# An mLSTM cell and a tanh-shrink MLP on one core: the filler matmuls before the first scores, and the densities in a list schedule

## The chip, the cores and the metric

The kernel runs on one core of a Trainium2 chip. The time is device microseconds of one execution, and the number compared is the median over several runs. A profiled execution has a span (first to last instruction) and a time of its own that is a little longer.

## The reference

First an mLSTM cell over 768 steps, for 4 sequences with 8 heads of 40 features; its output, 3072 tokens of 320 features, then goes through an MLP with 2048 hidden features whose activation is h - tanh(h).

```python
# q, k, v, o_gate: (4, 8, 768, 40); i_gate, f_gate: (4, 8, 768)
for t in range(S):
    m_new = maximum(f_gate[t] + m, i_gate[t])
    f_stab, i_stab = exp(f_gate[t] + m - m_new), exp(i_gate[t] - m_new)
    C = f_stab * C + i_stab * outer(v[t], k[t])        # (B, H, D, D)
    n = f_stab * n + i_stab * k[t]
    denom = maximum(abs(n . q[t]), 1.0)
    y[t] = sigmoid(o_gate[t]) * (C q[t]) / denom
x = y.transpose(0, 2, 1, 3).reshape(3072, 320)
h = x @ w_in                                            # (320, 2048)
out = (h - tanh(h)) @ w_out                             # (2048, 320)
```

## The kernel before

**The cell.** The 768 steps are cut into six chunks of 128, so with four sequences there are 24 units; unit n is chunk n // 4 of sequence n % 4. Each unit goes through the same operations. `scores` are 8 products of kz and qz into the PSUM banks `a0` and `a1`. VectorE masks them into P (two operations, tile `P`). `second` is 8 products of P with the scaled values vs (tile `ph`), and from the second chunk on also three products with the carried state. `gate` divides by the denominator and multiplies with the sigmoid of o (tiles `den`, `o`, `ys`). `turn` transposes the unit's y on TensorE (tile `px`), ScalarE copies it into xT, and `update` makes the new state from k and vs (tile `pc`). The gate sequences of the first two chunks are made ready first: a scan on VectorE, four transposes on TensorE and two products with triangles of ones (tile `gate`).

**The MLP.** Two units make a group of 256 tokens, and w_in and w_out are cut into eight pairs of blocks. They are stored in 64 bits and are converted on VectorE and ScalarE (tiles `w_e`, `w_m`, `w_r`). An item is one or two (group, pair) combinations: `ph_up` products with w_in, the activation on ScalarE and VectorE (tiles `z`, `q`, `gt`), and the way down (`po`, or `pS` in a form with seven products).

**The order.** Twelve units, the conversions and the MLP items of the first four groups are ordered by a list scheduler in the kernel's own text, the class `Plan`. Each `plan.add` gives an operation an engine, an assumed duration, what it comes after, a rank, tokens for buffers and banks, and a density `dense`. The order it finds is fixed on TensorE, VectorE and ScalarE: each instruction is chained behind the one before it on its engine. The DMA queue of SyncE (SP) isn't chained. There the framework places the transfers, and every transfer also waits for the one that used its completion semaphore eight before it, so that at most eight transfers of SP and ScalarE together are under way. From unit 12 on the order is a fixed pattern.

**Ones.** A matrix of ones (`diag`, bf16) is used for filler: `awake` and `stream` issue 128x512 matmuls whose result nobody reads. When `Plan.run` finds TensorE idle between two operations, `idle` fills the gap with as many as fit by the planner's clock. `share` adds up the densities of what TensorE did in the last `SPAN` us; when an operation of low density would bring this under `FEW`, denser work is taken first or ones are put in. `COLD` is the planner's assumption on how long TensorE runs slowly at the start.

**The loads.** For units 0 and 1 the loads stand ahead of everything else. The loads of later units are operations of engine "S" in the plan. The transfer of kz for unit 2 has one more wait: it goes behind the last TensorE instruction that had been recorded when the planner reached it.

```python
u[name] = plan.add("S", us, lambda: [load_unit(n, (name,), behind=[T.last] if n == 2 and name == "kz" else ()), arrive(n)], of(*after) + of(n - 1, name), rank + LATE.get(name, 0.0) + 2.0 * (n < 2), at=6.0 + 8.0 * (n < 2), kb=kb)
```

Of the kernel before, what the change touches and what calls it, by code (L numbers as in the profile page):

```python
# [79 lines left out]
def kernel(  # L80
# [77 lines left out]
    class Plan:  # L158
# [4 lines left out]
        LAG = {"T": 0.25, "V": 0.07, "A": 0.12, "S": 1.7, "G": 1.9, "N": 1.7}  # L163
        RATE, SHARED, COLD, TURN, WAIT = 0.3, 28.0, (12.0, 1.8), 0.12, 0.0364
        FEW, SPAN = 0.48, 2.6

# [176 lines left out]


    probe = const.tile([128, 1], FP, name="probe")
    V.memset(probe, 0.0)
# [5 lines left out]
    ones = const.tile([128, TOP], FP, name="ones")  # L352
    diag = const.tile([128, H, L], BF, name="diag")
# [10 lines left out]
    V.memset(ones, 1.0)  # L364
    V.memset(diag[:, HH:H], 1.0)

# [567 lines left out]
    PLANNED = 12  # L934
    SCALED, SHARED = (2, 4, 5, 6, 7, 11), (2, 4, 5, 6, 10, 11)
    RANKS = (-1.0, -1.0, -0.9464, 0.1262, 2.0044, 0.8216, 4.0244, 3.1226, 4.4155, 7.4293, 5.3654, 7.7018)
    WEIGHTS = (0.08, 0.0673, 1.9556, 3.3287, 6.8826, 8.3015, 4.4893, 6.619)
    START = item(FIRST * NP)
    HOLD = 32.6427
    plan = Plan(small=("b0", "b1"), a=1, up=1, po0=1, po1=1, gt=2, z=1, s4=1, P=4, vs=4, w64a=2, w64b=2, w=2, ob=2)  # L940

    def gates(c0, c1, rank, at, banks_of, after=()):
# [10 lines left out]
        def add(engine, us, name, after, take=None, give=None):  # L953
# [41 lines left out]
    units = {}  # L995
    LATE = {"o": -0.0338, "k": -2.3312}

    def plan_unit(n, rank):
# [26 lines left out]
        def first_part():  # L1025
# [9 lines left out]
        u["mask"] = [plan.add("V", 0.62, lambda i=i: ready[1][i](), [u["scores"]], rank - 0.621, give=[("a", held)] if i else ())  # L1035
                     for i in range(2)]
# [14 lines left out]
        for j, heads in enumerate(parts):  # L1051
            op = plan.add("T", 0.223 * len(heads) + (0.22 if c else 0.0), lambda j=j, heads=heads: second_part(j, heads),
                          ([op] if op else [u["prep"], u["column"], *before, *of(n, "q2") * (c > 0)]) + (u["mask"] if c else u["mask"][j:j + 1]), rank,
                          take=() if op else [("small", held)], give=[("P", held)] if j == len(parts) - 1 else (), dense=0.35)
        u["second"] = op
        if shared:
            steps = []
            over = plan.add("V", 0.6, lambda: [steps.extend(gate(n, in_parts=True)), steps[0]()], [op], rank - 1.4012)
            shares = plan.add("A", 1.9, lambda: steps[1](), [over, u["open"]], rank + 0.9389)
            u["gate"] = plan.add("V", 0.5, lambda: steps[2](), [shares, *of(n - 2, "turn")], rank - 3.6979, give=[("small", held)])  # L1060
        else:
# [15 lines left out]
        u["x"] = plan.add("A", 0.5, lambda: keep_x(n), [u["turn"]], rank - 3.4037, give=[("small", held_x)])  # L1077
        late = rank + (2.5552 if c else 1.5639)
# [6 lines left out]
    def plan_weights(p, rank, at):  # L1085
        for k, block in enumerate(blocks_of(p)):
            fetch, parts, low, power, one, sign, product = block
            held, r, buffer = {}, rank + 0.7421 * k, "w64" + "ab"[k]
            op = plan.add("G", 0.6 if k else 2.2, lambda fetch=fetch: fetch(begun[-1:]), begun_in_plan[:], r, [(buffer, held)], at=at, kb=655)
# [7 lines left out]

    plan.free["T"] = 1.6
    plan_gates(0, -2.0, 3.2, in_small)
# [4 lines left out]
    for n in range(2, PLANNED):  # L1104
        if n == 2 * B:
            plan_gates(1, 4.0679, 30.0, in_po)
        plan_unit(n, RANKS[n])
# [5 lines left out]
    for p in range(SPLIT, NP):  # L1113
        steps = []
        op = None
        for i in range(2):
            op = plan.add("V", 0.65, lambda p=p, i=i, steps=steps: [steps.extend([] if i else sums_of_weights(p)), *[step() for _, step in steps[2 * i:2 * i + 2]]],
                          [op] if op else [converted[p, 1], *([made[p - 1]] if p % 2 else [converted[n, k] for n in range(1, NP) for k in range(2)])], 0.2073 + 1.0 * p)
        made[p] = op

    def plan_item(x):

        run_of, some = items[x], tuple(run[:2] for run in items[x])
        n, rank = len(some), 2.2103 + 0.4005 * x
        held, got = {}, []
# [21 lines left out]

        op = plan.add("T", 0.43 * n, rest, [op], rank, tiles=2)

# [7 lines left out]
        for i in range(2):  # L1157
            z.append(plan.add("A", 0.3 + 0.25 * n, lambda i=i: square(i), [op, *z], -2.8126, () if i else [("z", held), ("gt", held)]))
        q = [plan.add("A", 0.2 + 0.25 * n, lambda i=i: got[2][1](i), [z[i]], -0.4608) for i in range(2)]
        cube = [plan.add("V", 0.15 + 0.27 * n, lambda i=i: got[2][2](i), [z[i]], -6.2574, give=[("up", held)] if i else ()) for i in range(2)]  # L1160
        g = [plan.add("V", 0.15 + 0.27 * n, lambda i=i: got[2][3](i), [q[i], cube[1]], -3.6973, give=[("z", held)] if i else ()) for i in range(2)]
        shrunk = g
        seven, (group, pair) = in_seven(*some[0]), some[0]
        if seven:
            g = [plan.add("V", 0.8 * n, lambda: sums_of_g(some), g[-1:], -3.0, [("w", held), ("s4", held)])]
        if x == START - 1:
            return
        if seven:
# [15 lines left out]
            for k, (cost, do, need) in enumerate(((0.82 * n, begin_run, [*shrunk, *sums_ready]),  # L1184
                                                  (0.54 * n, lambda: [step() for _, step in steps[3 * n + 1:5 * n + 1]], g),
                                                  (0.54 * n, lambda: [step() for _, step in steps[5 * n + 1:7 * n + 1]], []))):
                downs.append(plan.add("T", cost, do, need + downs[-1:] + [converted[p, 1] for _, p in some], rank + 0.4226,
                                      [("po0", mine), ("po1", mine), (name, mine)] if k == 0 and pair == SPLIT else (),
# [7 lines left out]
        for k, run in enumerate(run_of):  # L1196
            product, evict = down(k, some, *run, evict_at_once=False)
            first, last = run[1] == run[2], run[1] == run[3]
            for tt in range(GT):
                key = (run[0], run[2], tt)  # L1200
                po_held = runs.setdefault(key, {})
                done = plan.add("T", 1.08, lambda tt=tt, product=product: [product(i, tt) for i in range(2)],
                                g + downs[-1:] + [converted[run[1], 1]] + ([po_held["last"]] if "last" in po_held else []), rank + 0.4226,
                                [(f"po{tt}", po_held)] if first else (), [("gt", held)] if k == n - 1 and tt == GT - 1 else ())
# [275 lines left out]
```

## Time and profile before

| what | value |
|---|---|
| median of three runs | 544.16 us (542.82, 544.16, 552.6) |
| profiled execution, its own time | 542.34 us |
| its span | 540.1 us |
| mean granted TensorE clock | 0.982 |
| TensorE matmuls busy | 530.6 us, 98% |
| VectorE busy | 351.0 us, 65% |
| ScalarE busy | 200.7 us, 37% |
| matmuls of ones (`awake`) | 21, of which 18 before the first `ph_up` |
| first `ph_up` | at 27.22 us |

The table is read from the top down: TensorE is nearly always busy, so the span is the sum of what it does, of the few gaps in it and of the time in which its clock was lower. A matmul of float32 shows as two rows (two passes), so that 8 products are "x16".

### The profile page before, as it was taken

The page shows a single profiled execution, that of the slowest core. Times are in us where ns is not written, and L with a number is a line of the kernel's source. Part 1 is how long each engine was busy: PE and PEld are TensorE (multiplying, and loading weights), DVE is VectorE, ACT ScalarE, POOL GpSimd, SP SyncE. Part 2 cuts the span into 40 slices and gives each one's busy share as a digit, 9 for nine tenths or more (in the row PEclk, how much of TensorE's full clock was granted, in tenths as well). Part 3 has the DMA queues.
Part 4 walks back from the last instruction along what each step waited for, and adds up shares of the span by engine and source line. Part 5 has one row for each costly group of instructions (what it writes and reads, how often), then busy time and mean ns, then how long its engine had stood idle before and what let it go on. Part 6 is the DMA issues. An engine that isn't in the chain of part 4 may idle for free.

```text
span 540.1 us, 9214 instructions
## 1 busy us (share of the span) xinstructions
PE 530.6 (98%) x3475; PEld 461.9 (86%) x3475; DVE 351.0 (65%) x758; ACT 200.7 (37%) x534; POOL 26.9 (5%) x51
## 2 busy tenths in 40 slices
PE   7999999999999999999999999999999999999995
PEld 5788888888888989889999998998899899888873
DVE  5599999999764757855753854755655646553421
ACT  4458777454523423223213312322242242232321
POOL 4320212100000000000000000000000000000000
PEclk8599999999999999999999999999999999999999
DMA  7977653631001202021220310210200000000000
GB/s 226 278 236 224 208 169 103 184 100 53 13 1 37 62 26 76 27 64 32 81 53 24 92 58 26 74 50 26 72 16 12 1 25 0 2 25 0 26 0 30
DMA packets 28043, 37.98 MB, mean 70 GB/s; under 512 B 3736, under 2 KB 21720, under 8 KB 27992
## 3 DMA queue, kind: packets, MB, share of 16 engines
q1 hardware_dynamic: 21296, 22.24, 14.0%
q0 software_dynamic: 3040, 10.82, 6.5%
q10 hardware_dynamic: 3656, 4.26, 2.3%
q8 instruction: 29, 0.48, 0.4%
q14 instruction: 22, 0.18, 0.1%
HBM read 33.37 MB, written 3.93 MB: 69 GB/s over the span
## 4 chain that ended last, share of the span: by engine, by line
PE 98%; DMA 1%; SPq 0%; DVE 0%; issue 0%; ACT 0%; DVEq 0%
PE ph_up L130 41%; PE pS L130 26%; PE ph L130 10%; PE po L130 10%; PE ps L130 4%; PE pc L130 2%; PE px L134 2%; PE awake L130 1%; DMA kz<-in_kT 1%; PE gate L130 0%; SPq L303 0%; DVE P L107 0%; PE gate L134 0%; ACT ob L107 0%; SPq L322 0%
## 5 line engine op out<-in xcount | busy, mean ns | idle before, releaser
L130 PE MATMUL ph_up<-xT,w_in 128*128 128x256 f32 (+1 forms) x1152 | 245.0, 391 | 0.1
L130 PEld LDWEIGHTS ph_up<-xT,w_in 128*128 128x128 f32 (+1 forms) x1152 | 169.1, 189 | 29.2 <-issue 12.1
L107 ACT ACTIVATE z<-ph_up 128x512 f32<-128x512 f32 (+1 forms) x98 | 56.8, 584 | 261.8 <-issue 147.3
L107 DVE SCALAR_TENSOR_TENSOR gt<-ph_up,z 128x512 f32<-128x512 f32 (+1 forms) x98 | 62.6, 674 | 76.9 <-ACT z L107 76.9
L107 DVE TENSOR_TENSOR P<-ps,upto 128x512 f32<-128x512 f32 x48 | 31.6, 683 | 66.8 <-PE ps L130 66.7
L130 PE MATMUL pS<-wT,s 128*128 128x160 f32 x432 | 65.8, 300 | 0.0
L130 PEld LDWEIGHTS ph<-vs,P 128*128 128x128 f32 x384 | 60.6, 202 | 5.3 <-issue 0.9
L107 ACT ACTIVATE q<-z,tiny 128x512 f32<-128x512 f32 (+1 forms) x98 | 64.7, 709 | 0.0
L107 DVE SCALAR_TENSOR_TENSOR gt<-q,gt 128x512 f32<-128x512 f32 (+1 forms) x98 | 62.7, 672 | 0.2 <-ACT q L107 0.2
L130 PEld LDWEIGHTS pS<-wT,s 128*128 128x128 f32 x432 | 60.8, 190 | 0.0
L130 PE MATMUL ph<-vs,P 128*128 128x41 f32 x384 | 58.6, 272 | 0.0
L130 PE MATMUL po<-w_out,gt 128*128 128x320 f32 x192 | 56.4, 440 | 0.0
L130 PE MATMUL pS<-w_out,gt 128*128 128x160 f32 x288 | 51.1, 310 | 0.0
L130 PEld LDWEIGHTS po<-w_out,gt 128*128 128x128 f32 x192 | 35.0, 190 | 14.3 <-issue 1.7
L130 PEld LDWEIGHTS pS<-w_out,gt 128*128 128x128 f32 x288 | 41.6, 193 | 2.8 <-issue 2.3
L130 PEld LDWEIGHTS ps<-qz,kz 40*128 40x128 f32 x384 | 26.9, 199 | 4.5 <-issue 2.5
L130 PE MATMUL ps<-qz,kz 40*128 40x128 f32 x384 | 28.2, 287 | 1.5 <-DMA kz<-in_kT 1.5
L107 DVE TENSOR_TENSOR s<-gt 128x256 f32<-128x256 f32 x72 | 27.1, 419 | 0.0
L130 PE MATMUL pS<-wT,gt 128*128 128x160 f32 x144 | 26.3, 301 | 0.0
L130 PE MATMUL pS<-w_out,s 128*128 128x160 f32 x144 | 25.4, 299 | 0.0
L130 PE MATMUL ph<-state,q 120*128 120x123 f32 (+1 forms) x120 | 23.8, 279 | 0.0
L130 PEld LDWEIGHTS ph<-state,q 120*128 120x128 f32 (+1 forms) x120 | 20.4, 191 | 2.8 <-issue 0.7
(92 smaller groups left out, 455.4 us busy)
## 6 DMA issues: line engine op xcount, KB each, us to landing
w<-in_moe_w_out POOLq DMA_DIRECT2D x8, 640.0 KB, 6.5
w<-in_moe_w_in POOLq DMA_DIRECT2D x16, 256.0 KB, 4.9
kz<-in_kT SPq DMA_DIRECT2D x48, 80.0 KB
o<-in_o_gate SPq DMA_DIRECT2D x24, 160.0 KB
out<-ob ACTq DMA_DIRECT2D x24, 160.0 KB
k<-in_k SPq DMA_DIRECT2D x20, 180.0 KB
qz<-in_qT SPq DMA_DIRECT2D x44, 80.0 KB
v<-in_v SPq DMA_DIRECT2D x22, 160.0 KB
```

The source lines that it names most:

```text
L107: i = method(*args, **kwargs)
L130: return cls.keep(nc.tensor.matmul(*args, **kwargs))
L134: return cls.keep(nc.tensor.transpose(*args, **kwargs))
```

## The change

It has four parts. `diag` is filled first on VectorE, only its first 128 columns, and the ones read these 128 columns four times over instead of 512 different ones. The planner's constants are changed: TensorE is free from 1.1 instead of 1.6, the slow start is assumed to end at 5.8 instead of 12.0, the gap filler takes the whole gap in the first 2 us, qz of unit 0 is taken to arrive at 5.9 instead of 4.7, and `FEW`, `SPAN` and `WAIT` move. Operations have new densities: 0.2 for the gate preparation, 0.4 for scores, 0.32 for the second products, 0.7 for the half-height `ph_up`; operations with a rank of -2 or less are let through without ones. All ranks, dues and offsets have new values.

```diff
-        RATE, SHARED, COLD, TURN, WAIT = 0.3, 28.0, (12.0, 1.8), 0.12, 0.0364
-        FEW, SPAN = 0.48, 2.6
+        RATE, SHARED, COLD, TURN, WAIT = 0.3, 28.0, (5.8, 1.8), 0.12, 0.1012
+        FEW, SPAN = 0.52, 2.8
...
-                    if t > self.COLD[0] and op["dense"] < 0.6 and self.share(t, op["us"], op["dense"]) < self.FEW:
+                    if t > self.COLD[0] and op["dense"] < 0.6 and op["rank"] > -2.0 and self.share(t, op["us"], op["dense"]) < self.FEW:
...
+    diag = const.tile([128, H, L], BF, name="diag")
+    V.memset(diag[:, 0], 1.0)
     probe = const.tile([128, 1], FP, name="probe")
...
-    V.memset(diag[:, 0:HH], 1.0)
...
-    V.memset(diag[:, HH:H], 1.0)
...
-        row = diag.rearrange("p h t -> p (h t)")
         for _ in range(n):
-            T.matmul(bank, row[:, 0:128], row[:, 0:512], start=True, stop=True)
+            T.matmul(bank.rearrange("p (h t) -> p h t", h=HH), diag[:, 0], diag[:, 0:1].to_broadcast([128, HH, L]), start=True, stop=True)
...
-    SCALED, SHARED = (2, 4, 5, 6, 7, 11), (2, 4, 5, 6, 10, 11)
-    RANKS = (-1.0, -1.0, -0.9464, 0.1262, 2.0044, 0.8216, 4.0244, 3.1226, 4.4155, 7.4293, 5.3654, 7.7018)
-    WEIGHTS = (0.08, 0.0673, 1.9556, 3.3287, 6.8826, 8.3015, 4.4893, 6.619)
+    SCALED, SHARED = (2, 4, 7, 8, 9, 10, 11), (0, 2, 4, 6, 11)
+    RANKS = (-1.0, -1.0, -1.2849, 0.4084, 1.7142, 2.2823, 4.041, 4.6174, 0.2261, 11.3611, 9.05, 9.3515)
+    WEIGHTS = (0.08, -1.1577, 0.0935, 3.4541, 11.5093, 15.6285, 3.8529, 15.8989)
...
-    HOLD = 32.6427
+    HOLD = 9.9293
...
-            op = plan.add(engine, us, step, after, rank, [(names[take], mine)] if take is not None else (), [(names[give[0]], mine)] if give else ())
+            op = plan.add(engine, us, step, after, rank, dense=0.2, take=[(names[take], mine)] if take is not None else (), give=[(names[give[0]], mine)] if give else ())
...
-    LATE = {"o": -0.0338, "k": -2.3312}
+    LATE = {"o": 2.1402, "k": -3.6117}
...
-            u["qz"] = plan.add("N", 0.0, lambda: arrive(n), at=(4.7, 7.0)[n] - 1.7)
+            u["qz"] = plan.add("N", 0.0, lambda: arrive(n), at=(5.9, 7.0)[n] - 1.7)
...
-        u["scores"] = plan.add("T", 1.0, first_part, [u["qz"], *(of(n - 2, "second") if n in (2, 3) else [])], rank, [("a", held), ("P", held)], tiles=2, hold=HOLD * (n // B))
+        u["scores"] = plan.add("T", 1.0, first_part, [u["qz"], *(of(n - 2, "second") if n in (2, 3) else [])], rank, [("a", held), ("P", held)], tiles=2, hold=HOLD * (n // B), dense=0.4)
...
-                          take=() if op else [("small", held)], give=[("P", held)] if j == len(parts) - 1 else (), dense=0.35)
+                          take=() if op else [("small", held)], give=[("P", held)] if j == len(parts) - 1 else (), dense=0.32)
...
-                               at=0.0 if c else 36.8024 if n < 2 else 15.4905, dense=0.5)
+                               at=0.0 if c else 0.0 if n < 2 else 57.5308, dense=0.5)
...
-    plan.free["T"] = 1.6
+    plan.free["T"] = 1.1
...
-        n = int((t1 - t0) * share / one)
+        n = int((t1 - t0) * (1.0 if t0 < 2.0 else share) / one)
```

More of the change, by code (lines that the diff above doesn't have):

```diff
@@ L352 @@
     ones = const.tile([128, TOP], FP, name="ones")
-    diag = const.tile([128, H, L], BF, name="diag")
     rebias = const.tile([128, 1], FP, name="rebias")
@@ L1033, in plan_unit @@
         ready, held = [], {}
-        u["scores"] = plan.add("T", 1.0, first_part, [u["qz"], *(of(n - 2, "second") if n in (2, 3) else [])], rank, [("a", held), ("P", held)], tiles=2, hold=HOLD * (n // B))
-        u["mask"] = [plan.add("V", 0.62, lambda i=i: ready[1][i](), [u["scores"]], rank - 0.621, give=[("a", held)] if i else ())
+        u["scores"] = plan.add("T", 1.0, first_part, [u["qz"], *(of(n - 2, "second") if n in (2, 3) else [])], rank, [("a", held), ("P", held)], tiles=2, hold=HOLD * (n // B), dense=0.4)
+        u["mask"] = [plan.add("V", 0.62, lambda i=i: ready[1][i](), [u["scores"]], rank - 3.3795, give=[("a", held)] if i else ())
                      for i in range(2)]
@@ L1057, in plan_unit @@
             steps = []
-            over = plan.add("V", 0.6, lambda: [steps.extend(gate(n, in_parts=True)), steps[0]()], [op], rank - 1.4012)
-            shares = plan.add("A", 1.9, lambda: steps[1](), [over, u["open"]], rank + 0.9389)
-            u["gate"] = plan.add("V", 0.5, lambda: steps[2](), [shares, *of(n - 2, "turn")], rank - 3.6979, give=[("small", held)])
+            over = plan.add("V", 0.6, lambda: [steps.extend(gate(n, in_parts=True)), steps[0]()], [op], rank - 1.4854)
+            shares = plan.add("A", 1.9, lambda: steps[1](), [over, u["open"]], rank + 10.6391)
+            u["gate"] = plan.add("V", 0.5, lambda: steps[2](), [shares, *of(n - 2, "turn")], rank - 6.3482, give=[("small", held)])
         else:
@@ L1076, in plan_unit @@
         u["turn"] = plan.add("T", 0.35, turns, [u["gate"]], rank, [("small", held_x)], dense=0.5)
-        u["x"] = plan.add("A", 0.5, lambda: keep_x(n), [u["turn"]], rank - 3.4037, give=[("small", held_x)])
-        late = rank + (2.5552 if c else 1.5639)
+        u["x"] = plan.add("A", 0.5, lambda: keep_x(n), [u["turn"]], rank - 2.0837, give=[("small", held_x)])
+        late = rank + (0.5499 if c else 0.8655)
         u["update"] = plan.add("T", 0.64, updates, [u["second"], u["k"]], late, [("small", held_c)], [("vs", held)],
-                               at=0.0 if c else 36.8024 if n < 2 else 15.4905, dense=0.5)
+                               at=0.0 if c else 0.0 if n < 2 else 57.5308, dense=0.5)
         u["state"] = plan.add("V", 1.0 if c else 0.5, lambda: keep_state(n), [u["update"], *before, *of_states[c]], late, give=[("small", held_c)])
@@ L1087, in plan_weights @@
             fetch, parts, low, power, one, sign, product = block
-            held, r, buffer = {}, rank + 0.7421 * k, "w64" + "ab"[k]
+            held, r, buffer = {}, rank + 2.9939 * k, "w64" + "ab"[k]
             op = plan.add("G", 0.6 if k else 2.2, lambda fetch=fetch: fetch(begun[-1:]), begun_in_plan[:], r, [(buffer, held)], at=at, kb=655)
@@ L1105 @@
         if n == 2 * B:
-            plan_gates(1, 4.0679, 30.0, in_po)
+            plan_gates(1, 5.7952, 30.0, in_po)
         plan_unit(n, RANKS[n])
@@ L1117 @@
             op = plan.add("V", 0.65, lambda p=p, i=i, steps=steps: [steps.extend([] if i else sums_of_weights(p)), *[step() for _, step in steps[2 * i:2 * i + 2]]],
-                          [op] if op else [converted[p, 1], *([made[p - 1]] if p % 2 else [converted[n, k] for n in range(1, NP) for k in range(2)])], 0.2073 + 1.0 * p)
+                          [op] if op else [converted[p, 1], *([made[p - 1]] if p % 2 else [converted[n, k] for n in range(1, NP) for k in range(2)])], -6.5503 + 1.6192 * p)
         made[p] = op
@@ L1123, in plan_item @@
         run_of, some = items[x], tuple(run[:2] for run in items[x])
-        n, rank = len(some), 2.2103 + 0.4005 * x
+        n, rank = len(some), 4.4178 + 0.5804 * x
         held, got = {}, []
@@ L1146, in rest @@
                 step()
-        op = plan.add("T", 0.43 * n, rest, [op], rank, tiles=2)
+        op = plan.add("T", 0.43 * n, rest, [op], rank, tiles=2, dense=0.7)
         def square(i):
@@ L1157, in plan_item @@
         for i in range(2):
[L1158 to L1161, printed above, removed]
+            z.append(plan.add("A", 0.3 + 0.25 * n, lambda i=i: square(i), [op, *z], -3.8841, () if i else [("z", held), ("gt", held)]))
+        q = [plan.add("A", 0.2 + 0.25 * n, lambda i=i: got[2][1](i), [z[i]], -5.7767) for i in range(2)]
+        cube = [plan.add("V", 0.15 + 0.27 * n, lambda i=i: got[2][2](i), [z[i]], -8.2655, give=[("up", held)] if i else ()) for i in range(2)]
+        g = [plan.add("V", 0.15 + 0.27 * n, lambda i=i: got[2][3](i), [q[i], cube[1]], -12.778, give=[("z", held)] if i else ()) for i in range(2)]
         shrunk = g
@@ L1164, in plan_item @@
         if seven:
-            g = [plan.add("V", 0.8 * n, lambda: sums_of_g(some), g[-1:], -3.0, [("w", held), ("s4", held)])]
+            g = [plan.add("V", 0.8 * n, lambda: sums_of_g(some), g[-1:], -4.7618, [("w", held), ("s4", held)])]
         if x == START - 1:
@@ L1186, in plan_item @@
                                                   (0.54 * n, lambda: [step() for _, step in steps[5 * n + 1:7 * n + 1]], []))):
-                downs.append(plan.add("T", cost, do, need + downs[-1:] + [converted[p, 1] for _, p in some], rank + 0.4226,
+                downs.append(plan.add("T", cost, do, need + downs[-1:] + [converted[p, 1] for _, p in some], rank + 0.7926,
                                       [("po0", mine), ("po1", mine), (name, mine)] if k == 0 and pair == SPLIT else (),
@@ L1202, in plan_item @@
                 done = plan.add("T", 1.08, lambda tt=tt, product=product: [product(i, tt) for i in range(2)],
-                                g + downs[-1:] + [converted[run[1], 1]] + ([po_held["last"]] if "last" in po_held else []), rank + 0.4226,
+                                g + downs[-1:] + [converted[run[1], 1]] + ([po_held["last"]] if "last" in po_held else []), rank + 0.7926,
                                 [(f"po{tt}", po_held)] if first else (), [("gt", held)] if k == n - 1 and tt == GT - 1 else ())
```

## The prediction

> **What bounds the kernel now.** I read the page first (busy shares, then the slices), then TensorE's timeline of the first 30 us, the clock in stretches, the DMA queue of SP, and last the transfers by queue. The page:
>
> ```profile
> span 540.1 us, 9214 instructions
> PE 530.6 (98%) x3475; PEld 461.9 (86%) x3475; DVE 351.0 (65%) x758; ACT 200.7 (37%) x534; POOL 26.9 (5%) x51
> PEclk8599999999999999999999999999999999999999
> DMA  7977653631001202021220310210200000000000
> ```
>
> TensorE is busy throughout. Only the first two slices (27 us) show a low clock, and there the DMA engines are full. The waits of TensorE add up to 3.6 us, all before 9 us. So the useful work after 27 us is fixed, and the change can gain or lose only in the start-up and in new gaps. TensorE there:
>
> ```profile
> 1.56 2.74 PE L130 MATMUL awake<-diag 128*128 128x512 bf16 x6 [1.56 <-DVE diag L107]
> 5.51 0.46 PE L130 MATMUL ps<-qz,kz 40*128 40x128 f32 x2 [1.21 <-DMA kz<-in_kT]
> 6.23 1.13 PE L130 MATMUL ps<-qz,kz 40*128 40x128 f32 x14 [0.26 <-DMA kz<-in_kT]
> ...
> 9.12 2.08 PE L130 MATMUL ps<-qz,kz 40*128 40x128 f32 x16
> ...
> 21.30 2.08 PE L130 MATMUL ps<-qz,kz 40*128 40x128 f32 x16
> ...
> 25.64 1.16 PE L130 MATMUL ps<-qz,kz 40*128 40x128 f32 x16
> ...
> 27.22 1.10 PE L130 MATMUL ph_up<-xT,w_in 128*128 128x256 f32 x4
> 28.16 1.87 PE L130 MATMUL ph<-vs,P 128*128 128x41 f32 x16
> ```
>
> A unit's scores take 2.08 us at 9.1 and 21.3, and 1.16 at 25.6: half clock against full. The same change stands in the stretches (PEclk is the column after the four engines):
>
> ```profile
> 8.00:10.00 2.00, 1.76 (x12) 1.67 (x14) 1.29 (x5) 0.64 (x4) 0.08 (x1) 0.59 0.92 272
> 24.00:26.00 2.00, 2.00 (x12) 0.97 (x12) 2.00 (x5) 1.40 (x5) 0.00 (x0) 0.64 0.77 255
> 26.00:28.00 2.00, 1.90 (x21) 1.43 (x18) 1.41 (x3) 1.73 (x4) 0.00 (x0) 1.00 0.69 215
> ```
>
> Finer stretches put the fall at 8.4 and the rise at 25.4. SP's queue, with the time at which each transfer is issued:
>
> ```profile
> 7.79 1.43 SPq L322 DMA_DIRECT2D kz<-in_kT x4
> ...
> 12.17 0.35 SPq L333 DMA_DIRECT2D o<-in_o_gate  x1
> 13.40 0.33 SPq L328 DMA_DIRECT2D k<-in_k  x1
> 14.55 1.94 SPq L322 DMA_DIRECT2D kz<-in_kT  x2
> ...
> 22.19 0.35 SPq L333 DMA_DIRECT2D o<-in_o_gate  x1
> 23.65 0.35 SPq L328 DMA_DIRECT2D k<-in_k  x1
> ```
>
> A transfer of SP is issued when the one eight before it has landed, so issue times are also landing times. The first kz half of unit 2, issued at 7.79, releases the pair at 14.55: 6.8 us under way. The kz halves of unit 4, issued at 14.55 and about 16.2, release 22.19 and 23.65: 7.6 us. From 4 to 30 us the queues moved:
>
> ```profile
> q1 hardware_dynamic: 2664, 3.32, 44.8%
> q0 software_dynamic: 1040, 3.54, 43.9%
> ```
>
> SP's queue gets 3.32 MB / 26 us = 0.128 MB/us while GpSimd's weights take as much.
>
> **The change, part by part.** *Ones up to the first scores.* Before, 6 ones end at 4.30 and TensorE waits until 5.51. After, 9 ones start near 1.1 (the fill of diag is first on VectorE and a quarter as long) and end at 1.1 + 9 x 0.427 = 4.9; then the four gate transposes, then scores 0, which need kz at 6.2 as before. The wait for kz covers all of it: worth nothing by itself. If the ones are slower with their repeated operand (not in the trace), the 1.3 us up to 6.2 cover a third more.
>
> *More ones later.* The program's order has 42 ones against 21, and before the first `ph_up` 39 against 18: 21 more, 4.6 us at full clock (0.217 each), 9.0 at half. Useful work that moves ahead of the first `ph_up`: 8 second products (1.71 us at full clock) and one update (0.61, from 12 rows in 1.23): 2.3 us. After it both have three ones and the same work; changes between kinds of products are 485 and 484. I cost the rest of the new ranks at nothing, covered by TensorE's full queue of item work; if the cover fails it is VectorE that is late (18.8 of 20 us busy at 80 to 100).
>
> *The load of kz for unit 2.* This term decides. Before it stands in SP's queue after o2 and half of qz3 (SP order: gates, kz0, kz1, o0, o1, qz2, o2, half qz3, kz2). After, the order reads gates, kz0, kz1, o0, o1, qz2, o2, **o3, k0, q2 of unit 4 (three), k1, one third of q2 of unit 5, v2**, then kz2, qz3, kz3. Its extra wait has moved to the last gate product (`gate` with `ones`), but it also waits for o3 and k0 to land. The transfers up to kz2 are 64 + 320 + 320 + 160 + 160 + 160 + 180 + 160 + 180 + 60 + 160 + 160 = 2084 KB. In the queue of before the 2084th KB is the end of kz4's first half (64 + 320 + 320 + 160 + 160 + 80 + 320 + 80 + 160 + 160 + 180 + 80), which landed at 22.19. Second way: o2 lands at 12.17, 1060 KB follow at 0.128: 20.5. Third: issue at 14.5 and 16.8 (o3 and k0 landed) plus 6.8 to 7.6: 21.3 to 24.4. I take 22.0, between 19 (weights ask for less) and 24.
>
> *What TensorE does until then.* Its order: gates, scores 0, two gate products (to 8.2), 5 ones, scores 1, 5 ones, second 0, 4 ones, **scores 2**. At half clock from 8.4: 8.2 + 2.1 + 2.0 + 2.1 + 3.3 + 1.7 = 19.4; at full clock 13.4. Either way it then stands at scores 2 until kz2 lands; queued behind are all of TensorE's work, and on VectorE the masks of unit 2 stand ahead of the last conversion step of w_in block 0, of y of unit 0 and of unit 1's denominator.
>
> *From kz2 to the first `ph_up`.* The gap leaves the clock low. Which work lifts it is uncertain: 9.1 to 21.3 (scores, second products, seven ones) did not; scores, four ones and a transpose between 21.3 and 25.4 did. So it rises between 4 and 10 us after 22.0; I take 6.9, after the four ones inside second 1. Half clock: scores 2.0 (24.0), half of second 1 1.6, 4 ones 1.7, the other half 1.6: 28.9. Full clock: scores 3 0.9, 3 ones 0.65, transposes 0.35, half of second 2 0.86, 4 ones 0.87, half 0.86, transposes 0.35, 5 ones 1.1, update 0.6: 35.4. VectorE keeps up: masks to 25.3, w_in 26.1, y of unit 0 26.5, y of unit 1 30.5, ahead of the transposes at 30.4 and 33.4.
>
> *Sum.* First `ph_up` 35.4 against 27.2: 8.2 later, 2.3 us more work done: **+5.9 us**. 542.34 + 5.9 = 548.2 for a profiled execution. The median of the runs shown lies 1.8 above the profiled one; I give **549**. With kz2 at 19 the same steps give +2.7 (rise 3.4 us earlier in the sequence), at 24 +8.
>
> [...]
>
> **The rivals.**
>
> *Gain: kz2 lands by the time TensorE asks for it, and the ones hold the clock.* Then scores 2 start at 13.4, and the same steps at full clock (10.0 us) put the first `ph_up` at 23.4: 27.2 - 23.4 + 2.3 = 6.1 us saved, 536; with kz2 at 17 it is 2.5 us, 540. For it: the first ones did bring the clock up (scores 0 ran fast at 6.2), and the added ones stand in the gaps where it fell. Against it: 820 KB more of SP's transfers than before (1924 against 1104) stand ahead of kz2, with the DMA share at 0.92 to 1.10 from 6 to 22 us.
>
> *Slower by more: the clock stays at half until the first `ph_up`.* Place: all from scores 2 on. Price: the 10.0 us of full-clock work take 20.0: `ph_up` at 42, 42 - 27.2 - 2.3 = +12.5, 555 in the profile and 556.5 in the median. It decides if no stretch after 22 us is denser than those of 11 to 21 us before, whose ones (seven in ten us) weren't enough. Against it: four ones inside second 1 and three after scores 3 are closer together.
>
> *The ones change nothing, and kz2 is hidden.* Then only the 2.3 us and the 4.6 to 9.0 us of added ones count against each other: 545 to 549. For it: before, kz2 landed at 16.2 and was used at 21.3, five us of slack; against it, 820 KB / 0.128 is 6.4 us, and TensorE now asks for it earlier.
>
> **How the numbers follow.** Forecast (scores 2 wait for kz2, +2.7 to +8, median 545 to 552): 0.60. Gain: 0.17. Clock low until `ph_up`: 0.11. Ones without effect, kz2 hidden: 0.12. The range 538 to 555 takes in the forecast, the last rival and the slower half of the gain. A measurement here tells about 2% (10.9 us) from no change: faster by that would need 533.3, below every case (0.02); slower, 555.0, is the clock rival's (0.09); the rest is 0.89.
>
> **What would show it.** Right: TensorE idle, or a `ps` row ended by DMA kz, of 2 to 9 us before 23 us; kz of unit 2 issued on SP at 13 to 17; first `ph_up` at 32 to 38 with 39 ones ahead of it; VectorE's `P` of unit 2 late by the same. Wrong: scores 2 before 18 us, clock at 1.00 from 10 to 20 us, or first `ph_up` before 27; or waits of TensorE after 40 us, which I put at none.

## The result, and the profile after

The changed kernel takes 553.48 us in the median of six executions (547.53 to 554.82), the kernel before 544.27 us beside it. The ratio is 1.0158, with a 95% interval of 1.0119 to 1.0198: slower, by less than 2%. Every ratio here leaves out the executions that lie more than 1.5% above the fastest of the same kernel: of the kernel before, which has two groups, near 543.8 and near 552.5 us (22 of the 80 that ran beside the experiments), that is the upper group but for one of 551.77, and of the changed kernel none of ten (547.5 to 555.4). Over all these executions the means are 546.2 and 552.2 us.

The profiled execution of the changed kernel is its fastest, 547.53 us with a span of 545.7. Its page, in the lines that were shown of before:

```profile
span 545.7 us, 9210 instructions
PE 536.2 (98%) x3496; PEld 464.0 (85%) x3496; DVE 351.3 (64%) x757; ACT 203.4 (37%) x534; POOL 27.4 (5%) x51
PEclk9799999999999999999999999999999999999998
DMA  7977465352101101110221211211110000000000
```

The low clock still stands in the first two slices (27.3 us), at 9 and 7 instead of 8 and 5. Before, half clock was on record from 8.4 to 25.4 us; here it is from 19.8 to 30.0, and the rows below run at half speed before about 13 us too, where the record reads 1.00. TensorE's busy time has grown by 5.6 us, as much as the span. TensorE's timeline:

```profile
1.13 4.02 PE L130 MATMUL awake<-diag 128*128 128x512 bf16 x9 [1.13 <-DVE probe L107]
6.09 2.37 PE L130 MATMUL ps<-qz,kz 40*128 40x128 f32 x16
11.54 1.81 PE L130 MATMUL ps<-qz,kz 40*128 40x128 f32 x16
18.66 1.76 PE L130 MATMUL ps<-qz,kz 40*128 40x128 f32 x16 [1.54 <-DMA kz<-in_kT]
25.47 2.08 PE L130 MATMUL ps<-qz,kz 40*128 40x128 f32 x16
34.22 1.93 PE L130 MATMUL ph_up<-xT,w_in 128*128 128x256 f32 x8
```

The four `ps` rows are the scores of units 0 to 3; 1.16 us is full clock, 2.08 half. The third waits 1.54 us for kz of unit 2, the only wait above 0.2 us after 6 us. Behind it the clock falls:

```profile
18.00:20.00 2.00, 1.34 (x16) 1.29 (x16) 0.32 (x1) 2.00 (x10) 1.80 (x4) 0.94 0.91 243
28.00:30.00 2.00, 2.00 (x10) 1.53 (x8) 2.00 (x6) 0.38 (x2) 0.00 (x0) 0.50 0.77 224
30.00:32.00 2.00, 2.00 (x17) 1.62 (x16) 0.97 (x3) 1.49 (x3) 0.00 (x0) 1.00 0.46 136
```

PEclk, the column after the engines, is 0.50 from 20 to 30 us. The first `ph_up` starts at 34.22 instead of 27.22, with 2.3 us more useful work done: 4.7 us, against 5.6 in the span (where the other 0.9 us goes was not traced). On SP's queue kz of unit 2 is issued at 13.62 (7.79 was the first half's issue before), and v of unit 3 at 20.19:

```profile
13.62 1.94 SPq L322 DMA_DIRECT2D kz<-in_kT  x2
...
20.19 0.35 SPq L333 DMA_DIRECT2D v<-in_v  x1
```

The second of these looks harmless here: VectorE takes v up at 30.65 after waiting 0.17 us.

### The profile page after: what moved, and what is told of

Same layout as the page of the kernel before. It is cut to its first block, busy times and chain, and to the rows that moved or that the text cites. A ratio compares the mean times of both kernels' runs of the same rounds, so it can differ in the third digit from the quotient of the medians.

```text
span 545.7 us, 9210 instructions
## 1 busy us (share of the span) xinstructions
PE 536.2 (98%) x3496; PEld 464.0 (85%) x3496; DVE 351.3 (64%) x757; ACT 203.4 (37%) x534; POOL 27.4 (5%) x51
## 4 chain that ended last, share of the span: by engine, by line
PE 95%; DMA 3%; SPq 0%; issue 0%; ACT 0%
PE ph_up L130 41%; PE pS L130 26%; PE po L130 10%; PE ph L130 9%; PE ps L130 4%; PE pc L130 2%; PE px L134 2%; DMA kz<-in_kT 2%; DMA o<-in_o_gate 1%; PE awake L130 1%; SPq L303 0%; PE gate L134 0%; SPq L322 0%; PE gate L130 0%; ACT ob L107 0%
## 5 line engine op out<-in xcount | busy, mean ns | idle before, releaser
L107 ACT ACTIVATE q<-z,tiny 128x512 f32<-128x512 f32 (+1 forms) x98 | 66.2, 710 | 0.6
L130 PEld LDWEIGHTS ph<-vs,P 128*128 128x128 f32 x384 | 59.4, 198 | 5.7 <-issue 0.8
L130 PEld LDWEIGHTS po<-w_out,gt 128*128 128x128 f32 x192 | 34.9, 190 | 14.4 <-issue 1.0
L130 PEld LDWEIGHTS ps<-qz,kz 40*128 40x128 f32 x384 | 28.1, 204 | 4.0 <-DVE w_e L107 2.0
L130 PE MATMUL pS<-w_out,s 128*128 128x160 f32 x144 | 25.4, 299 | 0.0
```

Source lines behind the costliest of these rows:

```text
L107: i = method(*args, **kwargs)
L130: return cls.keep(nc.tensor.matmul(*args, **kwargs))
```

## A second execution of the changed kernel

Six executions with one profile don't explain a median 6 us above that profile. So both kernels were run again unchanged.

> The kernel before, unchanged, for the clock of each single execution. [...] Load theory: the spread of the changed kernel comes from when its transfers land, and the kernel before, whose loads have slack, shows no second value tied to the clock.

The kernel before: 543.3 to 553.3 us in twelve, six of them above 552, ratio 0.9999 (0.9987 to 1.0011). The profile caught one of 553.26 us: scores at half speed, and with them the first `ph_up`, up to 45 us, where the execution of 542.34 us had the full clock from 25.4 us on. So in the one execution profiled of each group it is the clock's rise that differs. The page's clock line reads 9 in all 40 slices, against its own rows:

```profile
26.91 2.08 PE L130 MATMUL ps<-qz,kz 40*128 40x128 f32 x16
29.64 2.04 PE L130 MATMUL ph_up<-xT,w_in 128*128 128x256 f32 x4
```

The first four rows of `ph_up` took 1.10 us in the execution of 542.34 us. A granted clock of 1.00 ahead of the first change on record is thus no evidence; the durations are.

> The changed kernel unchanged, for the profile of another execution and the clock of each. Its first six were 547.5 (the one profiled), 550.3 and four at 553.3 to 554.8. Clock theory: these four had the clock low for longer; a profile of one shows scores of units 0 to 3 or more at 2.0 us each and first ph_up at 38 to 41, with the same order and the same kz2 wait or none (TensorE arrives later). Load theory: a profile of one shows kz2 landing later than 18.7 or new waits.

The changed kernel: 548.44, 550.25, 554.36 and 555.37 us, ratio 1.0133 (1.0050 to 1.0216). The profile is of the 554.36 us execution (span 552.5). TensorE, then VectorE, then the clock:

```profile
18.73 1.16 PE L130 MATMUL ps<-qz,kz 40*128 40x128 f32 x16
...
29.28 1.93 PE L130 MATMUL ph_up<-xT,w_in 128*128 128x256 f32 x8
33.64 1.51 PE L130 MATMUL pc<-vs,k 128*120 128x123 f32 x6 [2.44 <-DVE state L107]
```

```profile
30.02 0.49 DVE L107 TENSOR_TENSOR vs<-v,ei 128x320 f32<-128x320 f32 x1 [2.93 <-DMA v<-in_v]
...
30.93 1.51 DVE L107 SCALAR_TENSOR_TENSOR w_r<-w_m,w_r 128x640 f32<-128x640 f32 x2
32.36 0.82 DVE L107 SCALAR_TENSOR_TENSOR w_e<-w,w_e 128x640 int32<-128x640 int32 x1
33.10 0.49 DVE L107 TENSOR_TENSOR state<-pc,eT 120x328 f32<-120x328 f32 x1
```

```profile
34.00:36.00 2.00, 2.00 (x10) 1.77 (x11) 1.86 (x4) 0.00 (x0) 2.00 (x5) 0.50 0.74 196
52.00:54.00 2.00, 2.00 (x10) 1.70 (x9) 0.65 (x3) 1.28 (x4) 0.00 (x0) 0.50 0.35 102
54.00:56.00 2.00, 2.00 (x14) 1.68 (x13) 2.00 (x5) 0.86 (x2) 0.00 (x0) 0.96 0.00 0
```

Here the rows run at full speed from about 17 us on (five ones at 13.46 us still took 2.32 us, four at 17.77 us took 1.03), nothing waits for kz, and the first `ph_up` comes 4.9 us *earlier* than in the faster execution. Then TensorE stands for 2.44 us: the update of unit 1 needs the PSUM bank that `state` of unit 0 frees; `state` stands in VectorE's fixed order behind `vs` of unit 3; and that waits 2.93 us for v of unit 3, issued at 19.90 and landed at 30. The clock falls and stays at half from 33.7 to 54.2 us, in the MLP's dense work. Against the other execution: -4.9 + 2.4 + 20.5 / 2 = +7.8 us; the spans differ by 6.8. Of what was expected of this run, the load theory's new wait is there; a first `ph_up` at 38 to 41 us is not.

The theory to test: the start-up is paced by SP's queue and by the clock together. A TensorE that arrives early waits for kz of unit 2, kz of unit 3, or v of unit 3, and the clock then falls; one that is slow never waits. The rivals: one part alone (the ones, the wait on kz, the early updates) makes the loss.

## One part at a time

**The first nine ones alone**, in the kernel before:

```diff
+    diag = const.tile([128, H, L], BF, name="diag")
+    V.memset(diag[:, 0], 1.0)
...
+            T.matmul(bank.rearrange("p (h t) -> p h t", h=HH), diag[:, 0], diag[:, 0:1].to_broadcast([128, HH, L]), start=True, stop=True)
...
-            awake(n)
+            awake(n + 3 * (t0 < 2.0))
```

> The kernel before with the changed ones alone: diag first and 128 columns, the repeated operand, and 9 ones instead of 6 ahead of the first scores; all else in the order of before. Part-worth-nothing theory (the wait for kz covers it): within 1 us of before. [...] If a 9-matmul stream does hold the clock through scores 0, first ph_up comes before 27.2.

545.05 us, ratio 1.0019 (1.0008 to 1.0030): a small loss of some 1 us, where the prediction had nothing. Scores 0 wait for kz until 6.14 as they did, and the first `ph_up` stands at 27.62.

**The changed kernel without the ones after them:**

```diff
+        if n and t0 > 2.0:
+            return n * one
```

> The changed kernel with its order kept, but the 33 ones after the first nine not issued; the planner still counts them, so that nothing else moves in TensorE's order. Dead-weight theory (ones cost their 217 ns each and give nothing): first ph_up earlier by up to the 30 ones ahead of it, about 6 us or more at the clock it has, as far as waits don't take it back. Clock theory: the clock stays at half until the ph_up products, scores take 2.1 us each, first ph_up no earlier than 32, and the time is the changed kernel's within 3 us. Load theory: whatever the ones do, scores 2 wait for kz at 18 to 19 us, now for longer (3 us or more).

548.08 us, ratio 1.0095 (1.0069 to 1.0120). With all 33 later ones left out the kernel is no slower than with them. TensorE waits longer, and the first `ph_up` is at half speed:

```profile
18.05 0.77 PE L130 MATMUL ps<-qz,kz 40*128 40x128 f32 x2 [2.91 <-DMA kz<-in_kT]
...
33.63 3.62 PE L130 MATMUL ph_up<-xT,w_in 128*128 128x256 f32 x8
```

**The changed kernel with its later ones doubled up to the first `ph_up`** (72 in all):

```diff
-            awake(n)
+            awake(n * (2 if t0 > 2.0 else 1))
```

> The changed kernel with each group of ones after the first stream, up to the first ph_up, doubled (60 instead of 30), order and loads unchanged. Clock theory with ones as the cure: denser work in every interval, the clock rises by 13 us in nearly every execution and falls less often; the spread shrinks to 3 us and the median lies at 548 to 552. Dead-weight theory: 30 more ones cost 0.22 to 0.43 us each wherever TensorE isn't waiting, first ph_up 4 to 10 us later, median 556 to 562.

551.17 us, ratio 1.0135 (1.0112 to 1.0157). The median and the highest time are where the clock theory put them; the spread is 3.9 us. In the profile (548.06 us) the clock is up from 11 us on and never falls, and yet the first `ph_up` stands at 34.51: the time goes into the 30 ones (6.5 us) and into waits of 0.4 and 0.8 us at the scores of units 2 and 3. A full clock alone doesn't win the time back.

**The wait on kz of unit 2 taken away** (of the line that loads a unit, only the changed part is shown):

```diff
-load_unit(n, (name,), behind=[T.last] if n == 2 and name == "kz" else ())
+load_unit(n, (name,), behind=())
```

> The changed kernel with the extra wait of the kz transfer of unit 2 left out; its place in SP's queue is then right behind qz of unit 2, ahead of o2, o3, k0 and v2; TensorE's order is the same. Load theory (the delay is kz of unit 2): scores 2 no longer wait, first ph_up 2 us or more before the 34.2 of the changed kernel, profile 543 to 545, median lower by 2 to 4 us. Clock theory: the 1.5 us wait goes, but TensorE's second products and ones after it still run at half clock, first ph_up at 31 to 34, median lower by no more than 2 us.

547.81 us (541.72 to 553.35), ratio 1.0032 (0.9994 to 1.0069); the mean over all ten is 547.0 us, against 552.2 of the changed kernel's ten. The framework then puts kz of unit 2 near the head of the queue, and its scores start at 15.68 without a wait. The lack moves one unit on:

```profile
21.49 0.76 PE L130 MATMUL ps<-qz,kz 40*128 40x128 f32 x2 [1.95 <-DVE ys L107]
23.29 2.04 PE L130 MATMUL ps<-qz,kz 40*128 40x128 f32 x14 [1.04 <-issue]
```

These are the scores of unit 3, whose kz and qz now stand behind o3, k0, q2 and v2. The row names `ys`, which had ended 0.26 us before; SP's queue shows the load. The halves of kz were issued from 14.46 us on, and the transfers eight places behind them, which go when they have landed, are issued just before the two rows start:

```profile
14.46 1.54 SPq L322 DMA_DIRECT2D kz<-in_kT  x2
...
21.41 0.35 SPq L328 DMA_DIRECT2D k<-in_k  x1
23.26 1.52 SPq L322 DMA_DIRECT2D qz<-in_qT  x2
```

The clock falls at 21.3 and rises at 34.9, and in this profile (548.01 us) the first `ph_up` stands at 35.46: the early start that the load theory expected did not come. Taking the wait away brings back some 5 us of the mean, so the order of the loads is a large part of the loss, but this edit is not by itself a cure. It also moves more than kz of unit 2: the transfers behind it get other places as well.

## The order of the loads

**SP's transfers chained in the planner's own order**, as the other engines' instructions are:

```diff
+    Y = Pinned(nc.sync)
...
-            nc.sync.dma_start(out=to[:, c0 * L:c1 * L], in_=part[:, c0 * L:c1 * L])
+            Y.dma_start(out=to[:, c0 * L:c1 * L], in_=part[:, c0 * L:c1 * L])
...
-    def load_unit(n, names=("kz", "qz", "v", "k", "o", "q2"), queue=nc.sync, behind=()):
+    def load_unit(n, names=("kz", "qz", "v", "k", "o", "q2"), queue=Y, behind=()):
...
-load_unit(n, (name,), behind=[T.last] if n == 2 and name == "kz" else ())
+load_unit(n, (name,), behind=())
```

> The changed kernel with every transfer of SP chained behind the one before it, so that the queue runs in the planner's order (kz2, o2, qz3, kz3, v2, o3, k0, qz4, kz4 ...), and without the extra wait of kz2. With kz2 alone early, scores 3 became the next to wait (to 21.5 and 23.3 us, kz and qz of unit 3 behind o3, k0, q2, v2). Load theory: now scores 2 and 3 both find their data, no wait of TensorE after 7 us, first ph_up at 24 to 28 where the clock is up by 15 us, median 540 to 544, 4 us or more below the kernel with kz2 alone early. Clock theory: the data come in time but the time still depends on when the clock rises; executions spread over 5 us or more, median 543 to 549.

551.9 us, ratio 1.0137 (1.0081 to 1.0193): no better. But its profile (551.65 us) shows an early start and what becomes of it at their plainest:

```profile
26.28 1.93 PE L131 MATMUL ph_up<-xT,w_in 128*128 128x256 f32 x8
32.69 1.51 PE L131 MATMUL pc<-vs,k 128*120 128x123 f32 x6 [4.48 <-DVE state L107]
```

```profile
29.07 0.49 DVE L107 TENSOR_TENSOR vs<-v,ei 128x320 f32<-128x320 f32 x1 [4.44 <-DMA v<-in_v]
```

The first `ph_up` is at 26.28, earlier than before the change; then 4.48 us of waiting for the same chain (v of unit 3, `vs`, `state`, bank), and half clock from 32 to 49.

**In that order, v of unit 3 right behind v of unit 2:**

```diff
-load_unit(n, (name,), behind=())
+*[load_unit(m, (name,)) for m in ((2, 3) if (n, name) == (2, "v") else () if (n, name) == (3, "v") else (n,))]
```

> The changed kernel with the transfers of SP in the order in which the planner puts them (as in the run with that edit) and, further, v of unit 3 issued right behind v of unit 2, ahead of o of unit 3. Load theory (the wait of TensorE inside the first ph_up is for the state of unit 0, which VectorE takes up only behind vs of unit 3, and so behind v of unit 3, which landed at 29.1 to 30.6 us in the three profiles of this order of VectorE): v of unit 3 lands by 23 us, the wait of 2.4 to 4.5 us for DVE state falls below 0.5 us, the first ph_up stands at 25 to 27 us and the clock at full before it; median 540 to 545. Rival (the clock falls by itself in the stretch in which second products and ph_up alternate, whatever the loads do): no wait for state, yet the clock goes to half for ten us or more between 25 and 50, and the median stays at 548 to 553. Second rival (the transfer only moves the lack to another one: o3, k0 or q of unit 4 land later): a new wait of over 1 us of TensorE or VectorE before 40 us, median 546 to 551.

548.08 us (540.86 to 553.30), ratio 1.0045 (1.0012 to 1.0077). Against the run before it only this transfer was moved in the program, and the intervals don't meet; over all executions the means are 547.7 us (twelve) and 551.6 (four): the late v was worth some 4 us. The load theory's 540 to 545 was missed. The median lies at the first rival's 548, but the profile (548.60 us) doesn't show that rival's mechanism: the clock is at half from 7.4 to 31.3 us, ahead of the first `ph_up`, and full where second products and `ph_up` alternate. There is no wait for `state`, but with the first `ph_up` 9.6 us later than in the run before that says little; the next run shows it with an early start.

```profile
12.01 1.47 SPq L107 DMA_DIRECT2D v<-in_v  x2
```

```profile
26.00:28.00 2.00, 2.00 (x13) 1.92 (x13) 0.33 (x2) 0.00 (x0) 0.00 (x0) 0.50 0.88 256
```

```profile
35.29 0.76 PE L131 MATMUL pc<-vs,k 128*120 128x123 f32 x6
35.89 1.93 PE L131 MATMUL ph_up<-xT,w_in 128*128 128x256 f32 x8
```

In this execution TensorE is busy without a gap from 8 to 30 us (2.00 us in each of the eleven stretches of 2 us), and its clock is at half all that time (0.50 in each). What fills it (scores, second products and the 20 planned ones) doesn't lift it. So that TensorE is busy in the profile isn't enough to expect the full clock.

**The same with 6 more ones in each of the first two gaps:**

```diff
-            awake(n)
+            awake(n + (6 if 2.0 < t0 < 13.0 else 0))
```

> The run with v of unit 3 behind v of unit 2, with 6 more ones in each of the first two gaps behind scores 0 (11 and 11 in place of 5 and 5; 54 in all). That run had no wait of over 0.4 us on TensorE after 7 us, and yet its clock stood at half from 6.7 to 30.7 us in the profile; its times lay at 541 to 545, 548 and 553. Clock theory (nothing but the mix of work is left: ones, scores and second products with 5 ones in each gap do not lift the clock, denser ones do): the clock is full by 15 us and stays so, the first ph_up stands at 26 to 29 us, the times draw together and the median is 541 to 545, although the 12 ones cost 2.6 to 5.2 us by themselves. Rival (the clock is not decided by these ones, or the early start ends in another wait for loads as in the runs before): the median stays at 547 to 552, with a wait of over 1 us on TensorE before 40 us or a clock at half beyond 25 us.

544.94 us (543.03 to 548.64), ratio 1.0027 (1.0000 to 1.0054). The median is where the clock theory put it, and the times have drawn together; over all executions the mean is 545.6 us, and that of the kernel before beside it 546.7. The profile (548.15 us) shows the rival too, in one execution: the rows run at full speed from the scores of unit 0 on, the first `ph_up` is at 26.70, and now other loads are late.

```profile
6.11 1.16 PE L131 MATMUL ps<-qz,kz 40*128 40x128 f32 x16
...
7.68 2.54 PE L131 MATMUL awake<-diag 128*128 128x512 bf16 x11
...
26.70 1.93 PE L131 MATMUL ph_up<-xT,w_in 128*128 128x256 f32 x8
30.30 0.83 PE L131 MATMUL pc<-vs,k 128*120 128x123 f32 x6 [1.67 <-DMA k<-in_k]
...
44.39 0.87 PE L135 MATMUL px<-ident,ys 128*128 128x128 f32 x3 [3.87 <-DVE ys L107]
```

```profile
24.56 0.48 DVE L107 TENSOR_TENSOR vs<-v,ei 128x320 f32<-128x320 f32 x1
...
27.63 0.49 DVE L107 TENSOR_TENSOR state<-pc,eT 120x328 f32<-120x328 f32 x1
...
40.63 1.27 DVE L107 TENSOR_TENSOR_SCAN w_in<-w_out,w_in 32x512 f32<-32x512 f32 x1 [4.92 <-DMA w_out<-in_i_gate]
```

`vs` of unit 3 and `state` of unit 0 now run without a wait, though the start is as early as in the first run of this section: that lack is cured. The wait of 1.67 us for k left the clock up; in the one of 3.87 us it fell, at 43.3 us, and stayed at half until 50.1. That second wait is VectorE's: `ys` stands behind the scan of the next gates (their tiles are called `w_out` and `w_in`), which waited 4.92 us for a transfer issued at 34.26. The ratios of the last two runs overlap, and in the two profiles the clocks differ before the first added one is issued (7.68 us). So that the twelve ones help is suggested by the median and the highest times, and not shown.

**The updates of units 0 and 1 due at 36.8 again:**

```diff
-                               at=0.0 if c else 0.0 if n < 2 else 57.5308, dense=0.5)
+                               at=0.0 if c else 36.8024 if n < 2 else 57.5308, dense=0.5)
```

> The changed kernel with the updates of units 0 and 1 due from 36.8 us again instead of from 0.0, and nothing else: the planner then puts the first four products of ph_up ahead of both updates (54 ones in all instead of 42). Load theory: no wait of TensorE for DVE state inside the first ph_up; the kz wait of unit 2 stays as it is (up to 1.6 us); the executions of 553 to 555 us go, and the median is 546 to 549. Rival (the long executions come from the clock alone and not from the wait for state): median 551 to 554, with executions above 552 still among them.

557.2 us in the median of four (548.48 to 560.4), the slowest version of all; the ratio of 1.0141 (1.0088 to 1.0195) rests on two of them only, and over all four the mean is 555.8 us against 545.4 of the kernel before beside it. Both sides missed. The wait for `state` is gone, but the planner moved much else (54 ones), and the profile, of the slowest execution (560.4 us), has the worst wait on kz of all, 5.6 us in two steps, one for each half of kz, with the clock at half from 18.3 to 42.2:

```profile
19.06 0.76 PE L130 MATMUL ps<-qz,kz 40*128 40x128 f32 x2 [3.62 <-DMA kz<-in_kT]
21.76 2.04 PE L130 MATMUL ps<-qz,kz 40*128 40x128 f32 x14 [1.94 <-issue]
```

So this run doesn't separate the early update from the loads. It shows that the wait for `state` isn't needed for a long execution: here one on kz stands before the half clock.

**The kernel before with its later ones doubled up to the first `ph_up`** (33 in all), by the same edit as for the changed kernel:

> The kernel before with each group of ones after the first six, up to the first ph_up, doubled (24 instead of 12). Its executions were of two kinds, near 543.5 and near 552.5, the second with scores at half clock until 43 us. [...] Dead-weight theory: both kinds stay, each 3 to 5 us later.

> The kernel before with every later stretch of ones twice as long (33 ones instead of 21), once more, as the version that may beat both kernels: its first run had ten times from 541.25 to 547.02 and none of the 552 that six in twenty-six of the kernel before had. If the denser ones do away with the executions in which the clock stays at half until 43 us: no time above 548 in 12, median 542.5 to 544, ratio 0.995 to 1.000. If the first run was luck: two or three times at 551 to 554, median 543.5 to 545.

543.5 us, ratio 0.9969 (0.9932 to 1.0005), and 543.88 us, ratio 1.0008 (0.9980 to 1.0035). In both profiles (547.02 and 546.02 us) scores still run at half speed until 26 us and more, and the first `ph_up` stands at 32.07 and 31.52; the ones didn't bring an early clock. The median is that of the kernel before; what differs is the spread. None of 22 executions is above 549.3 us, where 22 of 80 of the kernel before are above 550; the mean over all is 544.2 against 546.2 us. In the ratio, no version is clearly faster than the kernel before.

## The accounts of five profiles

Against the profiled execution of the changed kernel (first `ph_up` at 34.22, span 545.7), with the order of TensorE's useful work the same in all. A half-clock stretch after the first `ph_up` is counted at half its length:

| profile | first `ph_up` | waits after it | half clock after it | sum | span |
|---|---|---|---|---|---|
| changed kernel again | -4.9 | 2.4 | 20.5 / 2 | +7.8 | +6.8 |
| SP in the planner's order | -7.9 | 4.5 | 17 / 2 | +5.0 | +4.2 |
| v of unit 3 behind v of unit 2 | +1.7 | 0 | 0 | +1.7 | +1.2 |
| the same with 12 more ones | -7.5 | 5.5 | 7 / 2 | +1.5 | +0.7 |
| changed kernel, 72 ones | +0.3 | 0 | 0 | +0.3 | +0.5 |

Every sum is within 1 us of the span; the run with kz of unit 2 early, in the same order, gives +1.2 against +0.5. The second and fourth row answer where an early start goes: 7 to 8 us won by 26 us are given back before 50 us, in waits on SP's queue and in the half clock that follows them. These are accounts of single executions. That the half clock comes of the wait is read from their order in time; the 1.67 us wait with no fall behind it shows that not every wait does it.

## Why the prediction was right, and where it was not

- *The range.* 553.48 us lies in 538 to 555, near its upper end. The central 549 was 4.5 us low, and the forecast's own 545 to 552 doesn't hold the median: that the range held it is owed to the room left for a rival, and in part to luck.
- *Where the change acts.* The start-up alone, and no wait of TensorE after 40 us: so it is in both profiles of the changed kernel.
- *kz of unit 2.* The prediction named the place: scores 2 wait for kz, sent behind o3, k0 and q. It was issued at 13.62 us, within the 13 to 17 given, and the first `ph_up` came within 32 to 38. The size was off: kz landed at 18.5 instead of 22.0, just outside the 19 to 24, because it took 4.9 us and not 6.8 to 7.6. The wait was 1.54 us, under the 2 to 9 given as a sign. One sign of being wrong nearly came, a clock of 1.00 from 10 to 20 us: the record reads 1.00 to 18 us and 0.94 after, though the rows were at half speed until about 13. In the second execution, with another clock, there was no wait for kz at all.
- *The clock after it.* Half clock until 28.9, predicted; until 30.0, found. The first `ph_up` at 35.4, predicted; at 34.22, found; +5.9 us against +5.6 in the span. In the profiled execution the sum holds, partly by errors of opposite sign: kz landed 3.5 us earlier than taken, and the clock rose 11.5 us behind that landing instead of 6.9. The 3.4 us by which the sum for kz at 19 moves the rise earlier are a term that no run shows: with kz landed at 18.5 the clock rose at 30.0, and the span grew by 5.6 us instead of that sum's 2.7.
- *From the profile to the median: the term that was mis-sized.* "The median of the runs shown lies 1.8 above the profiled one; I give **549**." For the changed kernel that distance is 5.95 us, because the execution that happened to be profiled is the fastest of its six. The 1.8 was taken over from the kernel before, and nothing in the changed kernel's own start-up stood behind it.
- *"I cost the rest of the new ranks at nothing".* This failed in the longer execution that was profiled (554.36 us), whose time is near the median. VectorE "keeps up" was worked out for masks, conversions and y; `vs` of unit 3 with its load, and `state` of unit 0 behind it, were not followed, though the early updates made TensorE wait for them. "If the cover fails it is VectorE that is late" was the right name, without a price.
- *The first nine ones* at nothing: about +1 us by themselves. *The 21 later ones:* with all the later ones left out, the time is not longer (1.0095 against 1.0158 and 1.0133); as placed they bring nothing.
- *The rivals.* The gain's early start is real in single executions (first `ph_up` at 29.28, and 26.28 with another queue), but is given back. (Its start of scores 2 at 13.4 us should read 13.8, half of 11.2 us behind 8.2.) The clock low until `ph_up` is nearest in time (555 and 556.5), but in the profile of 554.36 us the half clock comes after the first `ph_up`, not before it. That kz is hidden and the ones change nothing is so in that same profile as far as kz goes, at a time outside its 545 to 549. No case had an early clock that is lost in the dense work.
- *Open.* Which waits the other executions of the changed kernel had wasn't seen: two of ten were profiled. What in TensorE's work lifts the clock wasn't shown (scores, second products and 20 ones did not in 22 us of a busy TensorE), nor what the early updates alone are worth.

## What to carry to other kernels

When an order of work is tightened, follow each load and each buffer release to the instruction that will now ask for it sooner, VectorE's in-order queue included; in these profiles a start that was quicker than its loads paid for them twice, in the wait and in the clock after it (4.48 us and 17 us at half, in one of them). A start-up with a clock that can rise at several moments (at 25.4, 30.0, 31.3 and 42.2 us in four of the profiles) has several times, so one profile is one case of them: work out what the others would wait for before adding a constant to come to a median. More filler drew the executions of the kernel before together (33 ones instead of 21) without a clear gain in the ratio: look at all executions, and not at the median alone, to see what it does.

## What the runs showed of the hardware

- A wait of 2.4 us behind the first `ph_up` was followed by 20.5 us at half clock, with TensorE nearly always busy (0.89 us or more of each us from 34 to 54); one of 4.5 us by 17 us, and in one of 3.9 us the clock fell for 7 us. One of 1.7 us, in a profile with the clock up, was followed by none.
- TensorE was busy by the profile for 22 us on end (8 to 30 us) at a granted clock of 0.50, when what it did was scores, second products and 20 ones.
- The granted clock read 1.00 up to its first recorded change, even where the rows took half-speed times (2.08 us for 16 rows of scores at 26.91 us, against 1.16); a mean clock of 0.998 stood beside such a slow start, in the execution of 553.26 us.
